# Attention, soft MoE and squared-ReLU FFN on one core: two steps written at another place in the last stage

## The chip, the core and the metric

The kernel runs on one core of a Trainium2 chip. The core has five engines that matter here: TensorE (PE in the profile; its weight loads are listed apart as PEld), VectorE (DVE), ScalarE (ACT), GpSimd (POOL) and SyncE (SP, which issues the DMAs). The metric is the device time of one execution in microseconds (us), lower is better. Before the change three runs took 477.72, 477.78 and 479.6 us; their median is 477.78.

## The reference, cut to what matters

```python
# stage 1: chunked attention, stage 2: soft MoE (slot_out is 32 rows, c is 3072 x 32)
x = c @ slot_out                       # 3072 x 512
# stage 3: squared-ReLU FFN, d_model 512, d_ff 2048
h = x @ w_in
r = np.maximum(h, 0.0)
g = s * (r * r) + b
return g @ w_out
```

The first two stages end in 32 slot rows and in the weights `c` of every token over them. So `x @ w_in` is `c @ (slot_out @ w_in)`, and the kernel never forms `x`: it forms m = slot_out @ w_in (32 x 2048, kept in `mpack`) and multiplies the transposed `c` (kept in `cpack`) by it.

## The kernel before, in words

All names below are those of the last stage, the squared-ReLU FFN. Its work is cut into 128 items. An item n is one block of 384 tokens and one block f of 128 columns of w_in. For each item:

- `emit_h(n)` (line 825) is one matmul on PE: 128 columns of `mpack` times 384 columns of `cpack`, into a PSUM tile with the tag `s`.
- `emit_relu(n)`, `emit_sq(n)`, `emit_ghi(n)` (lines 831, 835, 839) run on ACT: relu out of PSUM, the square, and a rounded copy `ghi`.
- `emit_g(n)` (line 842) runs on DVE: the rest `glo` = square minus `ghi`.
- `emit_o` and `emit_o2` (lines 877 and 889) are nine matmuls on PE, three token tiles times `ghi`·`w_hi`, `glo`·`w_hi` and `ghi`·`w_lo`. They come LA = 3 items behind the item's own `ghi`.

PSUM tiles have tags. `s` has two banks that are handed out in turn, to the h of every item and to the sums of m (below). A bank is given out again once its last reader is done, so an h waits for the reader of the tile two before it:

```python
bufs = {"s": 2, "g": 2}.get(tag, 1)
```

Beside the items the stage converts weights. w_out arrives as raw words and is split into `w_hi[f]` and `w_lo[f]`; blocks of w_in are converted in the same way. One conversion has a step on ACT (`stage_a`, line 579) and up to six on DVE (`stage_d`: lines 589, 591, 593, 600, 791, 793), and for w_out the cast to `w_hi` between them (`stage_w` on ACT, line 798; for f = 0 line 941 on DVE). DVE's first step reads what ACT's wrote.

m is formed in blocks of 512 columns. Block 0 is formed ahead of the items by `m_part` (line 688) in three column ranges: `ha` (128 columns, bank `mpa`), `hb` (128, `mpb`) and `hc` (256, `mpc`). `m_split` brings a range into `mpack`: a cast on ACT (line 817), then on DVE the rest for the lower 64 rows (line 818). Blocks 1 to 3 are formed within the items 4, 26 and 34 (`M_AT`): in item n `emit_m` runs 8 or 12 matmuls in four column groups into one `s` bank (line 806) and copies it to `mps` on ACT (line 808). In item n + 1 `emit_m2` adds the four column groups with one fp32 matmul against a stacked identity (line 812, listed as two) into another `s` bank, and splits that into `mpack` (lines 817, 818).

There is no planner: every engine takes its instructions in the order in which the code writes them, and waits where an operand or a bank is not ready. Within one item of the loop PE's order is `emit_h(n)`, the nine o matmuls of earlier items, then the matmul of `emit_m` or `emit_m2` if there is one. For the items 5 to 7 the h stands behind the o matmuls. Raw tiles of w_in and w_out come by DMA into a ring of three; the first tile of w_out is the last transfer that the head of this stage needs.

Of the kernel before, what the change touches and what calls it, by code (L numbers as in the profile page):

```python
# [35 lines left out]
def kernel(  # L36
# [30 lines left out]
    def psum(tag, shape):  # L67
        bufs = {"s": 2, "g": 2}.get(tag, 1)
        return ps.tile(shape, F32, tag=tag, name=tag, bufs=bufs)
# [48 lines left out]
    with tc.manual_schedule():  # L118
# [457 lines left out]
        def cv_act(key, i, w):  # L576
            h, lf, a = (cvs[i][:, j, :] for j in range(3))
            cv[key] = h, lf, a, w
            nc.scalar.activation(out=h, in_=w[:, :, 1].bitcast(F32), func=AF.Copy, scale=2.0 ** -112)
# [22 lines left out]
        def wi_src(fb, j):  # L602
            w = wt["wi", 2 * fb + j // 2].rearrange("p (k f t) -> p (k f) t", k=KD, t=2)
            return w[:, 512 * (j % 2):512 * (j % 2) + 512, :]
# [81 lines left out]
        def m_part(mp, kcs, cols):  # L686
            for kc in kcs:
                nc.tensor.matmul(out=mp[:, cols], lhsT=soT4[:, kc].rearrange("p r s -> p (r s)"),
                                 rhs=wis_a[kc // 2][:, kc % 2, cols], start=(kc == 0), stop=(kc == KD - 1))
# [56 lines left out]
        M_AT = (4, 26, 34)  # L746
# [26 lines left out]
        def stage_a(k):  # L773
            key = cq.get(k)
            if key:
                if key[0] == "i":
                    w = wi_src(key[1], key[2])
                else:
                    w = wt[raw_of[key]].rearrange("p (f d t) -> p f d t", f=2, t=2)[:, key[1] % 2]
                cv_act(key, k // 2 % 2, w)  # L780

        def stage_d(k, j):
            key = cq.get(k)
            if key:
                h, lf, a, w = cv[key]
                if j < 3:
                    cv_dve(key, j)
                elif j == 3:
                    cv_low(key, lf if key[0] == "o" else wi_dst([wis_l[:, 0:2], wis_l[:, 2:4]], key))
                elif key[0] == "o" and j == 4:  # L790
                    nc.vector.tensor_tensor(out=a, in0=a, in1=w_hi[key[1]].bitcast(F32), op=ALU.subtract)
                elif key[0] == "o":
                    nc.vector.tensor_tensor(out=w_lo[key[1]], in0=a, in1=lf, op=ALU.add)
# [6 lines left out]
        def emit_m(fb):  # L800
            wis = wis_b if fb % 2 else wis_a
            mp = psum("s", [128, 512])
            for lo in range(1 if fb == 1 else 2):
                for kc in range(KD):
                    lhsT, rhs = (soTb[:, kc, :], wis_l[:, kc, :]) if lo else (soT4[:, kc, 0, :], wis[kc // 2][:, kc % 2, :])
                    nc.tensor.matmul(out=mp[32 * kc:32 * kc + 32, :], lhsT=lhsT, rhs=rhs,
                                     start=(lo == 0), stop=(lo == 1 or fb == 1))
            nc.scalar.copy(out=mps, in_=mp)

        def emit_m2(fb):  # L810
            mr = psum("s", [128, 512])
            nc.tensor.matmul(out=mr, lhsT=stks_all, rhs=mps, start=True, stop=True)
            m_split(mr, 512 * fb, slice(0, 512))

        def m_split(mp, base, cols):
            m = mpack[:, base + cols.start:base + cols.stop]
            nc.scalar.copy(out=m, in_=mp[:, cols])
            nc.vector.tensor_tensor(out=m[64:128], in0=mp[64:128, cols], in1=m[64:128].bitcast(F32), op=ALU.subtract)  # L818

        def emit_h(n):  # L820
            if n >= len(items):
                return
            (b, _, _), f = items[n]
            hq = psum("s", [128, UT])
            nc.tensor.matmul(out=hq, lhsT=mpack[:, 128 * f:128 * f + 128], rhs=cpack[:, b * UT:(b + 1) * UT],  # L825
                             start=True, stop=True)
            h_t[n] = hq

        def emit_relu(n):
            if n < len(items):  # L830
                nc.scalar.activation(out=r_g[n % 2], in_=h_t.pop(n), func=AF.Relu)  # L831
# [5 lines left out]
        def emit_ghi(n):  # L837
            if n < len(items):
                nc.scalar.copy(out=ghi_g[n % (LA + 2)], in_=r2_g[n % 2])  # L839
# [28 lines left out]
        def emit_o(n, parts=(0, 1)):  # L868
            r_, f = items[n]
            ghi, glo = ghi_g[n % (LA + 2)], glo_g[n % (LA + 2)]  # L870
            if f == r_[1] and 0 in parts:
                o_t[r_] = [psum(("pt", "x", "xt", "lp", "g", "g")[3 * place[r_] + t], [128, DM]) for t in range(NTU)]
            if n == len(items) - 1:
                return
            for gt in [(ghi, glo)[x] for x in parts]:
                for t in range(NTU):
                    nc.tensor.matmul(out=o_t[r_][t], lhsT=gt[:, 128 * t:128 * t + 128], rhs=w_hi[f],  # L877
                                     start=(f == r_[1] and gt is ghi), stop=False)

        def emit_o2(n):  # L880
            r_, f = items[n]
            b, f0, f1 = r_
            ghi, glo = ghi_g[n % (LA + 2)], glo_g[n % (LA + 2)]
            for t in range(NTU):
                o = o_t[r_][t]
                if n == len(items) - 1:
                    for gt in (ghi, glo):
                        nc.tensor.matmul(out=o, lhsT=gt[:, 128 * t:128 * t + 128], rhs=w_hi[f], start=False, stop=False)
                nc.tensor.matmul(out=o, lhsT=ghi[:, 128 * t:128 * t + 128], rhs=w_lo[f], start=False, stop=(f == f1 - 1))  # L889
                if f == f1 - 1:  # L890
                    if b < 4 and f0 == 0:
                        to = part[b][t] if b < 2 else os_early(b - 2, t)
                        if t == 1:
                            nc.scalar.activation(out=to, in_=o, func=AF.Copy, scale=sbt[:, 0:1])
                        else:
                            nc.vector.tensor_scalar(out=to, in0=o, scalar1=sbt[:, 0:1], scalar2=None, op0=ALU.mult)  # L896
                    else:
                        os_ = os_g[t]
                        nc.vector.scalar_tensor_tensor(out=os_, in0=o, scalar=sbt[:, 0:1], in1=part[b][t] if f0 else bias,
                                                       op0=ALU.mult, op1=ALU.add)  # L900
                        store(b, t, os_)
# [12 lines left out]
        def stages(n, *js):  # L914
            for j in js:
                stage_d(n, j)
# [10 lines left out]
            cp[k](out=soT4[:, 2 + k, :, 16:32].rearrange("p r (e j) -> p r e j", e=4),  # L927
                  in_=sot[:, k:k + 1, :, 0:4].to_broadcast([128, 4, 4, 4]))
        m_part(mpb, (0, 1), hb)
        stage_a(0)  # L930
        m_part(mpa, (2, 3), ha)
        m_split(mpa, 0, ha)
        m_part(mpb, (2, 3), hb)
        stages(0, 0)
        m_split(mpb, 0, hb)
        emit_h(0)
        emit_h(1)
        mpc = psum("g", [128, 512])
        m_part(mpc, range(KD), hc)
        stages(0, 1)  # L940
        nc.vector.tensor_copy(out=w_hi[0], in_=cv[cq[0]][2])
        act(0)
        emit_g(0)
# [25 lines left out]
        for n in range(LA + 1, len(items) + LA + 1):  # L969
            if n > 7:  # L970
                emit_h(n)
            m = n - LA - 1
            ends = 0 <= m and items[m][1] == items[m][0][2] - 1
            late = m + 1 < len(items) and m + 1 == 2 * HF + 1
            if ends or late:
                emit_o2(m)
            if 1 < m + 1 < len(items):
                emit_o(m + 1)
            if m > 1 and not ends and not late:
                emit_o2(m)  # L980
            if LA + 1 < n <= 7:
                emit_h(n)
            if n == 6:
                nc.vector.tensor_copy(out=soTb, in_=soT4[:, :, 0, :])
            emit_relu(n)
            emit_sq(n)
            stage_a(n + 1)
            emit_ghi(n)
            if n in M_AT:
                emit_m(M_AT.index(n) + 1)  # L990
            if n - 1 in M_AT:
                emit_m2(M_AT.index(n - 1) + 1)
            if LA + 1 < n <= len(items):
                emit_g(n - 1)
            stage_d(n, 1)
            stage_w(n)
            stages(n, 2, 3)
            stages(n - 1, 4, 5)
            stage_d(n + 1, 0)
            if 48 <= n < 64:  # L1000
                for i in (2 * n - 96, 2 * n - 95):
                    wsum_add(i)
            if n == 64:
                colsum()
            if 65 <= n < 77:
                add_bias(n - 65)
            while wnext[0] < len(order) and last_use.get(order[wnext[0] - NRG], -1) <= n:
                load_w(1)
# [72 lines left out]
```

## Time and profile before

| | before |
|---|---|
| median of 3 runs | 477.78 us |
| the profiled execution's own time | 481.1 us |
| its span in the trace | 479.3 us |
| PE busy (3960 matmuls) | 455.8 us, 95% |
| PE weight loads | 342.8 us, 72% |
| DVE busy | 309.6 us, 65% |
| ACT busy | 307.6 us, 64% |
| granted TensorE clock, mean | 0.999 |

The profiled execution took 3.3 us longer than the median of the runs. The span in the trace is 1.8 us shorter than that execution. The matmuls of one item are pipelined: their listed durations overlap, and it is the distance between the starts that says how fast PE goes. The items run from 171.9 us to the end.

### The profile page before, as it was taken

To read this page: it belongs to the slowest core of one execution; us is meant where nothing else is said; L and a number is where in the kernel's file an instruction comes from. 1 tells how busy PE (TensorE), PEld (TensorE's weight loads), DVE (VectorE), ACT (ScalarE), POOL (GpSimd) and SP (SyncE) were. 2 spreads that over 40 slices of the span, in tenths; PEclk is the share of its full clock that TensorE was granted. 3 is DMA by queue.
4 is the path that set the end of the run, shared out by engine and by line. 5 is a ranking of instruction groups with operands and counts; after the bars stand their busy time and mean duration, and the time that the engine had idled before them with its cause. 6 is when DMAs were issued, how large, how long until landed. Compare 5 with 4: busy or idle time off the path is not lost.

```text
span 479.3 us, 10204 instructions
## 1 busy us (share of the span) xinstructions
PE 455.8 (95%) x3960; PEld 342.8 (72%) x3960; DVE 309.6 (65%) x685; ACT 307.6 (64%) x635; POOL 84.1 (18%) x154
## 2 busy tenths in 40 slices
PE   6889998999999878999999999999999999999996
PEld 5656666665545365886787888887888888888885
DVE  5768888886485867999485999985624224223232
ACT  4556665665134357998686888666666666666660
POOL 6665655560000000000000000006700000000000
PEclk9999999999999999999999999999999999999999
DMA  8999999999999932333332000003101001001011
GB/s 302 371 406 403 399 408 401 392 384 402 384 408 383 416 137 88 116 150 96 115 142 88 1 1 0 1 0 131 69 0 67 0 1 66 0 1 65 2 66 66
DMA packets 20576, 83.04 MB, mean 173 GB/s; under 512 B 2736, under 2 KB 2864, under 8 KB 14640
## 3 DMA queue, kind: packets, MB, share of 16 engines
q1 hardware_dynamic: 20528, 82.39, 44.5%
q8 instruction: 31, 0.51, 0.4%
q14 instruction: 17, 0.14, 0.1%
HBM read 76.09 MB, written 6.29 MB: 172 GB/s over the span
## 4 chain that ended last, share of the span: by engine, by line
PE 68%; DVE 12%; DMA 10%; ACT 4%; issue 2%; POOL 2%; SPq 1%; DVEq 0%; POOLq 0%; ACTq 0%
PE g L877 11%; PE lp L877 5%; PE pt L877 5%; PE x L877 5%; PE g L889 5%; PE xt L877 5%; PE s L825 4%; DMA keys<-in_w_out_dram 4%; DMA vals<-in_vm_dram 3%; PE s L630 3%; PE x L325 3%; PE lp L889 3%; PE pt L889 3%; PE xt L889 3%; PE x L889 3%; PE s L285 2%
## 5 line engine op out<-in xcount | busy, mean ns | idle before, releaser
L842 DVE TENSOR_TENSOR glo<-r,ghi 128x384 fp32r<-128x384 f32 x128 | 76.3, 600 | 81.4 <-ACT ghi L839 81.2
L831 ACT ACTIVATE r<-s 128x384 f32<-128x384 f32 x128 | 62.7, 490 | 52.7 <-PE s L825 52.4
L835 ACT ACTIVATE r<-r 128x384 f32<-128x384 f32 x128 | 67.2, 525 | 9.7 <-DVE glo L842 5.6
L839 ACT CAST ghi<-r 128x384 fp32r<-128x384 f32 x128 | 65.4, 511 | 3.4
L825 PE MATMUL s<-cpack,mpack 128*128 128x384 f32 x128 | 44.7, 352 | 1.9 <-DVE mpack L818 1.9
L301 ACT ACTIVATE seg<-seg 128x384 f32<-128x384 f32 x32 | 28.7, 897 | 19.2 <-DVE seg L312 15.3
L889 PE MATMUL g<-wlo,ghi 128*128 128x512 f32 x128 | 40.2, 394 | 0.0
L877 PE MATMUL g<-whi,ghi 128*128 128x512 f32 x126 | 39.7, 394 | 0.3 <-DVE mpack L818 0.3
L877 PE MATMUL g<-whi,glo 128*128 128x512 f32 x126 | 39.4, 393 | 0.0
L864 POOL TENSOR_TENSOR keys<-keys,bias 128x512 f32<-128x512 f32 x6 | 8.4, 1430 | 169.4 <-DVE bias L853 169.4
L263 POOL TENSOR_SCALAR keys<-keys 64x416 f32<-64x416 f32 x63 | 33.6, 533 | 14.2 <-DMA keys<-in_kq_dram 7.4
L285 PE MATMUL s<-keys 128*32 128x128 f32 x768 | 30.3, 291 | 5.0 <-POOL keys L267 4.2
L325 PE MATMUL x<-vals,seg 128*32 128x128 f32 x744 | 28.0, 275 | 3.6 <-DMA vals<-in_vm_dram 2.9
L825 PEld LDWEIGHTS s<-cpack,mpack 128*128 128x128 f32 x128 | 23.9, 188 | 9.5 <-DVE mpack L818 2.0
L325 PEld LDWEIGHTS x<-vals,seg 128*32 128x32 f32 x744 | 20.5, 109 | 13.3 <-DVE seg L309 4.6
L889 PEld LDWEIGHTS g<-wlo,ghi 128*128 128x128 f32 x128 | 24.0, 188 | 5.2
L877 PEld LDWEIGHTS g<-whi,glo 128*128 128x128 f32 x126 | 23.7, 188 | 5.4
L285 PEld LDWEIGHTS s<-keys 128*32 128x32 f32 x768 | 19.5, 113 | 11.0 <-POOL keys L267 6.5
L319 ACT COPY seg<-pt 128x384 f32<-128x384 f32 x32 | 15.2, 476 | 18.5 <-PE pt L317 17.6
L877 PEld LDWEIGHTS g<-whi,ghi 128*128 128x128 f32 x126 | 23.7, 188 | 4.4 <-DVE mpack L818 0.7
L877 PE MATMUL lp<-whi,ghi 128*128 128x512 f32 x63 | 25.5, 404 | 0.9 <-DVE vals L896 0.9
L877 PE MATMUL pt<-whi,glo 128*128 128x512 f32 x64 | 25.3, 395 | 0.7 <-DVE glo L842 0.7
(255 smaller groups left out, 990.6 us busy)
## 6 DMA issues: line engine op xcount, KB each, us to landing
seg<-in_w_dram SPq DMA_DIRECT2D x27, 1024.0 KB, 8.5
keys<-in_kq_dram SPq DMA_DIRECT2D x32, 396.0 KB, 7.3
vals<-in_vm_dram SPq DMA_DIRECT2D x64, 192.0 KB, 6.6
keys<-in_w_in_dram SPq DMA_DIRECT2D x5, 1024.0 KB, 5.1
keys<-in_w_out_dram SPq DMA_DIRECT2D x5, 1024.0 KB, 4.9
out_dram<-os SPq DMA_DIRECT2D x18, 256.0 KB, 2.1
vals<-in_w_in_dram SPq DMA_DIRECT2D x3, 1024.0 KB, 7.7
vals<-in_w_out_dram SPq DMA_DIRECT2D x3, 1024.0 KB, 4.8
```

The costliest lines, as they stand in the source:

```text
L263: (nc.vector if h and u == 0 else nc.gpsimd).tensor_scalar(out=stream(kz[rows, h], 0, CH), in0=k[rows, UT * h:UT * h + (NCU + 1) * CH].rea ...
L285: nc.tensor.matmul(out=o, lhsT=qt[:, 32 * c:32 * c + 32], rhs=kz[:, :, at:at + WIN], start=True, stop=not (first or last))
L301: nc.scalar.activation(out=p_r[u], in_=sm_r[u].rearrange("p t h (a r) -> p t r (h a)", a=2), func=AF.Exp, scale=scale)
L319: nc.scalar.copy(out=pts_r[u], in_=pt)
L325: nc.tensor.matmul(out=xp[32 * r:32 * r + 32, t], lhsT=pts_r[u][:, 32 * c:32 * c + 32], rhs=vbuf[u // 2 % 2][:, u % 2, :, 64 * c:64 * c + ...
L825: nc.tensor.matmul(out=hq, lhsT=mpack[:, 128 * f:128 * f + 128], rhs=cpack[:, b * UT:(b + 1) * UT], start=True, stop=True)
L831: nc.scalar.activation(out=r_g[n % 2], in_=h_t.pop(n), func=AF.Relu)
L835: nc.scalar.activation(out=r2_g[n % 2], in_=r_g[n % 2], func=AF.Square)
L839: nc.scalar.copy(out=ghi_g[n % (LA + 2)], in_=r2_g[n % 2])
L842: nc.vector.tensor_tensor(out=glo_g[n % (LA + 2)], in0=r2_g[n % 2], in1=ghi_g[n % (LA + 2)].bitcast(F32), op=ALU.subtract)
L877: nc.tensor.matmul(out=o_t[r_][t], lhsT=gt[:, 128 * t:128 * t + 128], rhs=w_hi[f], start=(f == r_[1] and gt is ghi), stop=False)
L889: nc.tensor.matmul(out=o, lhsT=ghi[:, 128 * t:128 * t + 128], rhs=w_lo[f], start=False, stop=(f == f1 - 1))
```

## The change

Two places in the code are written in another order; no instruction is added or removed, and on PE, POOL and SP the order stays as it was.

```diff
         m_part(mpb, (0, 1), hb)
-        stage_a(0)
         m_part(mpa, (2, 3), ha)
         m_split(mpa, 0, ha)
         m_part(mpb, (2, 3), hb)
-        stages(0, 0)
+        stage_a(0)
         m_split(mpb, 0, hb)
         emit_h(0)
         emit_h(1)
         mpc = psum("g", [128, 512])
         m_part(mpc, range(KD), hc)
-        stages(0, 1)
+        stages(0, 0, 1)
...
+            if n in M_AT:
+                emit_m(M_AT.index(n) + 1)
+            if n - 1 in M_AT:
+                emit_m2(M_AT.index(n - 1) + 1)
             emit_relu(n)
             emit_sq(n)
             stage_a(n + 1)
             emit_ghi(n)
-            if n in M_AT:
-                emit_m(M_AT.index(n) + 1)
-            if n - 1 in M_AT:
-                emit_m2(M_AT.index(n - 1) + 1)
```

The first piece is DVE's order at the head of the stage. `mpack<-pt` and `mpack<-lp` are the rests of the ranges `ha` and `hb`; L589, L591 and the cast to `whi` (line 941 before, 940 now) are the first conversion of w_out.

```order
 L818 TENSOR_TENSOR mpack<-pt,mpack 64x128
-L589 TENSOR_SCALAR seg_99<-seg_99 128x512
 L818 TENSOR_TENSOR mpack<-lp,mpack 64x128
-L591 SCALAR_TENSOR_TENSOR seg_99<-keys,seg_99 128x512
-L941 CAST whi_2622<-seg_99 128x512
+L589 TENSOR_SCALAR seg_99<-seg_99 128x512
+L591 SCALAR_TENSOR_TENSOR seg_99<-keys,seg_99 128x512
+L940 CAST whi_2622<-seg_99 128x512
```

Both rests now stand ahead of the conversion. On ACT the conversion's step (L579) has likewise moved by one, from ahead of the cast of `ha` to between the casts of `ha` and `hb`.

The second piece is ACT's order in items 4 and 5. The three instructions relu, square and `ghi` of item 4 (r_2658, r_2660, ghi_2666) stood just ahead of its first row before.

```order
 L808 COPY mps_2657<-s 128x512
+L831 ACTIVATE r_2658<-s 128x384
+L835 ACTIVATE r_2660<-r_2658 128x384
+L839 CAST ghi_2666<-r_2660 128x384
 L798 CAST whi_2624<-seg_99 128x512
-L831 ACTIVATE r_2659<-s 128x384
-L835 ACTIVATE r_2661<-r_2659 128x384
-L579 ACTIVATE keys<-keys 128x512
-L839 CAST ghi_2662<-r_2661 128x384
 L817 CAST mpack<-s 128x512
+L831 ACTIVATE r_2659<-s 128x384
+L835 ACTIVATE r_2661<-r_2659 128x384
```

The copy to `mps` now stands ahead of item 4's three instructions, and the cast to `mpack` ahead of item 5's four.

The third piece is ACT's order in items 26 and 27 (r_2658 to ghi_2663 belong to item 26, r_2659 to ghi_2664 to item 27).

```order
-L831 ACTIVATE r_2658<-s 128x384
-L835 ACTIVATE r_2660<-r_2658 128x384
-L839 CAST ghi_2663<-r_2660 128x384
 L808 COPY mps_2657<-s 128x512
-L831 ACTIVATE r_2659<-s 128x384
-L835 ACTIVATE r_2661<-r_2659 128x384
-L579 ACTIVATE seg_99<-keys 128x512
-L839 CAST ghi_2664<-r_2661 128x384
+L831 ACTIVATE r_2658<-s 128x384
+L835 ACTIVATE r_2660<-r_2658 128x384
+L839 CAST ghi_2663<-r_2660 128x384
 L817 CAST mpack<-s 128x512
```

Copy and cast have moved ahead of the relu of the same item here too; items 34 and 35 show the same.

## Rows read from the trace of the kernel before

**Rows 1.** The page's chain that ended last: share of the span by engine.
```profile
PE 68%; DVE 12%; DMA 10%; ACT 4%; issue 2%; POOL 2%; SPq 1%; DVEq 0%; POOLq 0%; ACTq 0%
```

**Rows 2.** Stretches: length, then busy us (instructions) by engine, clock, DMA.
```profile
171.00:190.00 19.00, 15.99 (x67) 10.99 (x68) 15.21 (x29) 14.98 (x32) 0.00 (x0) 1.00 0.19 71
190.00:215.00 25.00, 25.00 (x112) 20.57 (x111) 24.41 (x48) 21.70 (x45) 0.00 (x0) 1.00 0.36 127
...
222.00:300.00 78.00, 78.00 (x355) 61.90 (x354) 63.54 (x118) 62.06 (x126) 0.00 (x0) 1.00 0.17 61
```

**Rows 3.** Timeline, ACT, head: start, length, instruction, [idle before <- what ended it].
```profile
170.74 0.66 ACT L579 ACTIVATE seg<-keys 128x512 f32<-128x512 f32 x1 [2.38 <-DMA keys<-in_w_out_dram]
171.31 0.25 ACT L817 CAST mpack<-pt 128x128 fp32r<-128x128 f32 x1
```

**Rows 4.** Timeline, DVE, head of the stage.
```profile
171.59 0.29 DVE L818 TENSOR_TENSOR mpack<-pt,mpack 64x128 fp32r<-64x128 f32 x1 [2.58 <-ACT mpack L817]
...
172.37 0.29 DVE L818 TENSOR_TENSOR mpack<-lp,mpack 64x128 fp32r<-64x128 f32 x1
172.70 0.69 DVE L591 SCALAR_TENSOR_TENSOR seg<-keys,seg 128x512 int32<-128x512 int32 x1
...
174.04 0.56 DVE L842 TENSOR_TENSOR glo<-r,ghi 128x384 fp32r<-128x384 f32 x1 [0.19 <-ACT ghi L839]
```

**Rows 5.** Timeline, ACT, items 3 to 5.
```profile
179.54 0.48 ACT L831 ACTIVATE r<-s 128x384 f32<-128x384 f32 x1
...
181.60 0.47 ACT L831 ACTIVATE r<-s 128x384 f32<-128x384 f32 x1
...
183.09 0.58 ACT L808 COPY mps<-s 128x512 f32<-128x512 f32 x1
184.14 0.62 ACT L798 CAST whi<-seg 128x512 fp32r<-128x512 f32 x1 [0.47 <-DVE seg L591]
...
186.57 0.58 ACT L817 CAST mpack<-s 128x512 fp32r<-128x512 f32 x1
```

**Rows 6.** Timeline, PE and PEld, 180 to 189 us.
```profile
180.07 0.16 PEld L806 LDWEIGHTS s<-vals,keys 128*32 128x32 f32 x8 [0.40 <-ACT r L831]
...
183.72 1.13 PE L812 MATMUL s<-mps,stk 128*128 128x512 f32 x2 [0.82 <-ACT mps L808]
...
188.50 0.50 PE L877 MATMUL pt<-whi,glo 128*128 128x512 f32 x1 [0.70 <-DVE glo L842]
```

**Rows 7.** Timeline, DVE, item 5.
```profile
184.60 0.69 DVE L600 SCALAR_TENSOR_TENSOR seg<-keys,seg 128x512 f32<-128x512 uint32 x1
187.18 0.69 DVE L818 TENSOR_TENSOR mpack<-s,mpack 64x512 fp32r<-64x512 f32 x1 [1.89 <-ACT mpack L817]
```

**Rows 8.** Timeline, PE and ACT, items 26 to 28.
```profile
235.87 0.40 PE L806 MATMUL s<-seg 128*32 128x512 bf16 x4
236.19 0.44 PE L825 MATMUL s<-cpack,mpack 128*128 128x384 f32 x1
236.31 0.59 ACT L808 COPY mps<-s 128x512 f32<-128x512 f32 x1 [1.70 <-PE s L806]
...
236.47 0.40 PE L877 MATMUL pt<-whi,ghi 128*128 128x512 f32 x1
...
236.79 0.50 ACT L831 ACTIVATE r<-s 128x384 f32<-128x384 f32 x1
...
238.53 1.02 PE L812 MATMUL s<-mps,stk 128*128 128x512 f32 x2
...
239.57 0.39 PE L877 MATMUL lp<-whi,ghi 128*128 128x512 f32 x1
239.59 0.59 ACT L817 CAST mpack<-s 128x512 fp32r<-128x512 f32 x1 [0.79 <-PE s L812]
```

**Rows 9.** Instructions of line 825: ns min/median/max, first and last start.
```profile
L825 PEld LDWEIGHTS s<-cpack,mpack x128: 186/188/190, 171.9 to 465.9; 128*128 128x128 f32 x128
```

**Rows 10.** Timeline, PE, the end of the first run of items.
```profile
219.68 0.50 PE L877 MATMUL lp<-whi,ghi 128*128 128x512 f32 x1 [0.86 <-DVE vals L896]
```

## The prediction

> **What bounds the kernel now.** I read the chain of waits first, because it says which engine's time sets the end: 68% of it is PE, 12% DVE, 10% DMA [rows 1]. An average over a whole span hides stages, so I then cut the last stage into stretches [rows 2]. From 171 to 190 us no engine is full: PE is busy for 15.99 of 19 us, DVE for 15.21. From 190 to 215 us PE is full (25.00 of 25) and DVE nearly (24.41). From 222 to 300 us PE is full again (78.00 of 78), and it stays so. The timelines say what ends each idle piece. At the head ACT waits until 170.74 for the first tile of w_out [rows 3]. In items 4 and 5 PE and DVE wait for ACT's copy and cast of m: PE 0.82 and, by way of `glo`, 0.70 us [rows 6], DVE 1.89 us [rows 7]. At 219.68 PE waits for DVE once more [rows 10]. After that an instruction moved on ACT can only matter if PE comes to wait for it.
>
> The granted clock is 1.00 in all these stretches [rows 2], the ones with PE's waits included, so I give the clock no term.
>
> **The head.** Before, ACT began the first conversion step at 170.74 and the cast of `ha` at 171.31, 0.57 later [rows 3]. DVE took the rest of `ha` at 171.59, 0.28 after the cast, and the rest of `hb` at 172.37, between two conversion steps; the next step began at 172.70, and `glo` at 174.04 after 0.19 of idle [rows 4]. Now the cast of `ha` is done while ACT waits for the DMA, and the cast of `hb` takes its place at 171.31. DVE takes the rest of `hb` at about 171.59, where that of `ha` stood. The second rest thus leaves the series: 172.70 − 172.37 = 0.33 us. The 0.19 of idle goes too, because h and relu of item 0 no longer wait for a cast behind the DMA. Together 0.5 us. The DMA itself is not sooner, so there is no more to gain: ACT's step still starts at 170.74. What follows on DVE up to item 4 is nearly a closed series, so the 0.5 us is carried on. Bounds: 0 (if item 0's `ghi` is late again) to 0.7; I take 0.5.
>
> **Items 4 and 5.** All times are before's; the 0.5 is counted above. ACT's relu of item 4 began at 181.60 [rows 5]. The matmuls of `emit_m` had run from 180.07 with nothing behind them on that bank [rows 6], so the copy to `mps` can take this place: 181.60 to 182.19 instead of 183.09. Then relu, square and `ghi` of item 4 end about 0.58 later than they did, still ahead of the cast of `whi` at 184.14, which waits for DVE [rows 5]: nothing late there. PE's sum (L812) no longer waits for `mps`: its 0.82 goes, less some 0.1 because h of item 5 now needs the later relu. The cast to `mpack` follows `whi` directly. That one ends at 184.14 + 0.62 = 184.76, so the cast begins at about 184.7 in place of 186.57 and ends at about 185.3. DVE's rest can start when L600 ends, 184.60 + 0.69 = 185.29, in place of 187.18: 1.89 us less [rows 7]. The `glo` behind it, for which PE waited 0.70 at 188.50 [rows 6], moves by the same. relu, square, conversion step and `ghi` of item 5 come 0.58 later; DVE's conversion series is far enough behind (its next first step needs the rest, a `glo` and two w_out steps first) that nobody waits for them.
>
> Is the 1.89 worth its size at the end? Over 190 to 215 us PE runs without a gap, so it gains only if it enters that run sooner. It does: its idle pieces before 190 are the 0.82, the 0.70 and the restart behind them, and the 0.5 of the head. At 219.68 DVE sets PE's start [rows 10], and DVE is sooner by 0.5 + 1.89. Gain at the two early places: 2.4 us. Bounds: 0.5 (only the head) to 3.3 (if the 0.86 at 219.68 goes as well).
>
> **Items 26 and 34.** Here PE is full, and ACT waits for PE, not PE for ACT [rows 2, 8]. PE's order is h(26), nine o, the matmuls of `emit_m`, h(27), nine o, L812, h(28). The `s` banks go in turn: h(26) one, `emit_m` the other, h(27) the first again, L812 the other, h(28) the first. So h(27) waits for relu(26), and h(28) for relu(27). Before, both were long done. Now relu(26) stands behind the copy, and the copy behind the last matmul of `emit_m`.
>
> First wait. The copy starts at 236.31 as before. The next relu starts 0.48 later (236.79) [rows 8]. A bank is free 0.53 after its relu's start: relu at 179.54 [rows 5], the weight load that waited for it at 180.07 [rows 6]. So h(27) starts at 236.31 + 0.48 + 0.53 = 237.32 instead of 236.19: 1.13 us. Queued behind it are the nine o matmuls, and nothing else can go ahead.
>
> Second wait. L812 to the cast is 239.59 − 238.53 = 1.06, cast to relu 0.48, relu to bank 0.53, h to the next o 236.47 − 236.19 = 0.28: together 2.35 us from L812 to the next o. Before it was 239.57 − 238.53 = 1.04 [rows 8], since h(28) was pipelined into the sum. So 1.31 us.
>
> That is 2.44 us per place. Items 34 and 35 have the same pattern (the copy's idle of 1.70 stands there again), so 4.9 us. The copy's and cast's own gain here is worth nothing: PE's order puts their next use nine matmuls or more later. DVE's rest of m comes 1.1 later together with all PE work, and DVE has idle time there (63.54 of 78 us busy [rows 2]). Bounds: 0, if the relus were never needed in time, to 6, if a start after each wait costs another 0.25 us.
>
> In the row at 180.07 the weight load itself was held until relu was done [rows 6]. The Trainium skill, TensorE: Matmul & The Clock Gate, section Step-by-step: what each phase is for, says that the queue can pull a weight load ahead of running matmuls. By that rule the load of h (0.188 us [rows 9]) would lie inside each of the four waits, at most 0.75 us less, and the sum would be +1.8 instead of +2.5. I go by the row.
>
> **The sum.** −0.5 − 1.9 + 4 waits (2 × 1.13 + 2 × 1.31 = 4.9) = +2.5 us. Against the profiled execution: 481.1 + 2.5 = 483.6. The median of the runs lies 3.3 below that execution; I put the same difference on it: 477.78 + 2.5 = 480.3 us.
>
> **Rivals.**
> - The early gain is lost in the full stretch. PE has no gap from 190 to 215 [rows 2]; if its restart there is set by something that did not move, only the head's 0.5 counts: 477.78 + 4.9 − 0.5 = 482.2. Against it: every idle piece of PE that the rows name before 190 ends with something that moves. 0.14.
> - Only one wait per late place. If h(28) finds its bank free (say, relu(27) gets done before L812 has drained), 2 × 1.31 falls away: 477.7. Against it: ACT's order puts the cast, which needs L812's result, ahead of that relu. 0.14.
> - Faster: the late places cost nothing. The mechanism would be that PE has slack there, the stretch being paced by DVE's conversions (63.54 of 78 us busy, in bursts). Then only the 2.4 shows: 475.4; it decides itself at h(27), 1.13 us or none. Against it: PE busy for 78.00 of 78. 0.06.
> - The change does less at the head than it says, since the first tile's DMA rules: 0.5 less, 480.8. It lies within the forecast's own range.
>
> **How the numbers follow.** Forecast 0.60 (own range 479.2 to 481.4), the three rivals 0.14, 0.14, 0.06, and 0.06 for a mixture. About 0.5% (2.4 us) is what a measurement of this kernel can tell from no change, so the borders are 475.4 and 480.2; the forecast sits on the upper one, and I split its 0.60 into 0.30 slower and 0.30 within. Slower: 0.30 + 0.14 + some 0.05 of the mixture = 0.49. Faster: 0.04, since that rival lies on the lower border. Within: 0.47. Range 477.6 to 482.4: it takes in both middle rivals and leaves out the faster one.
>
> **What would show it.** In the trace after: the rest of `hb` at about 171.6 and `glo` 0.5 sooner; no idle of DVE ahead of its next L818, and PE's L812 in item 5 without a wait for `mps`; PE's run without gaps beginning some 2.4 us sooner than 190; then at the two late places h waiting for ACT's relu, twice each, with 1.1 and 1.3 us. Wrong would be: a PE without these four waits, or an early part that arrives at 222 us with less than 2 us in hand.

## The result and the profile after

The changed kernel takes 480.65 us (median of 21 runs), the kernel before 478.0 us (21 runs). The ratio is 1.0052, with a 95% interval from 1.0035 to 1.0068: 2.5 us slower, between 1.7 and 3.3. The prediction was 480.3 us, 2.5 us more than the 477.78 it started from.

The profiled execution after is one of the shorter ones: 479.52 us, span 477.7, which is less than the 479.3 of before. The spans of two single executions can't be set against each other here, because the weight transfers end at different times: PE was done with the range `ha` of m at 169.64 us in the trace of before and at 167.19 in that of after. So I compare intervals within each trace.

**The early items.** ACT and DVE in items 4 and 5 of the changed kernel (start, length, engine, line, instruction, idle time before it):

```profile
177.66 0.57 ACT L808 COPY mps<-s 128x512 f32<-128x512 f32 x1
178.12 0.49 ACT L831 ACTIVATE r<-s 128x384 f32<-128x384 f32 x1
...
180.20 0.62 ACT L798 CAST whi<-seg 128x512 fp32r<-128x512 f32 x1 [0.48 <-DVE seg L591]
180.72 0.58 ACT L817 CAST mpack<-s 128x512 fp32r<-128x512 f32 x1
```

```profile
180.66 0.69 DVE L600 SCALAR_TENSOR_TENSOR seg<-keys,seg 128x512 f32<-128x512 uint32 x1
181.36 0.69 DVE L818 TENSOR_TENSOR mpack<-s,mpack 64x512 fp32r<-64x512 f32 x1
```

The rest of m follows the conversion step without a gap; its 1.89 us of idle in [rows 7] is gone. PE's sum no longer waits either; the row that had 0.82 in [rows 6] now reads:

```profile
178.80 1.02 PE L812 MATMUL s<-mps,stk 128*128 128x512 f32 x2
```

From the first `w_lo` on DVE to h(8) on PE it takes 11.53 us, and 13.43 in the trace of before: 1.90 us less.

**The late items.** ACT in items 26 and 27, then PE, in the changed kernel; they answer to [rows 8]:

```profile
230.52 0.59 ACT L808 COPY mps<-s 128x512 f32<-128x512 f32 x1 [3.54 <-PE s L806]
231.00 0.50 ACT L831 ACTIVATE r<-s 128x384 f32<-128x384 f32 x1
...
234.56 0.59 ACT L817 CAST mpack<-s 128x512 fp32r<-128x512 f32 x1 [1.96 <-PE s L812]
235.04 0.50 ACT L831 ACTIVATE r<-s 128x384 f32<-128x384 f32 x1
```

```profile
230.08 0.40 PE L806 MATMUL s<-seg 128*32 128x512 bf16 x4
231.16 0.45 PE L825 MATMUL s<-cpack,mpack 128*128 128x384 f32 x1 [0.68 <-ACT mps L808]
...
233.50 1.02 PE L812 MATMUL s<-mps,stk 128*128 128x512 f32 x2
235.59 0.44 PE L825 MATMUL s<-cpack,mpack 128*128 128x384 f32 x1 [1.07 <-ACT r L831]
235.88 0.39 PE L877 MATMUL lp<-whi,ghi 128*128 128x512 f32 x1
```

Both waits of h are there. The second is as forecast: from L812 to the next o 235.88 − 233.50 = 2.38 us (forecast 2.35, before 1.04). The first is not: h(27) starts at 231.16, while relu(26), which began at 231.00, still runs. What it waited for is the copy, which ends at 230.52 + 0.59 = 231.11.

**The full stretches.** PE is busy for every microsecond from 184.2 to 209, as it was from 190 to 215 in [rows 2], and the clock is still 1.00 (columns: stretch, length, then busy time and instructions of PE, PEld, DVE, ACT, POOL, clock, DMA):

```profile
184.20:209.00 24.80, 24.80 (x111) 20.41 (x110) 24.21 (x47) 22.08 (x46) 0.00 (x0) 1.00 0.37 129
216.00:294.00 78.00, 74.50 (x336) 58.27 (x335) 60.17 (x111) 58.89 (x120) 0.00 (x0) 1.00 0.18 62
```

The later stretch lost 78.00 − 74.50 = 3.5 us of PE that was full before: the four waits (2 × 0.68 + 2 × 1.07). The idle time is counted from the listed ends of pipelined matmuls; by the starts of the h the waits cost more, 4.2 us (the late items alone, below). The wait at the end of the first run [rows 10] stands as it was:

```profile
213.87 0.50 PE L877 MATMUL lp<-whi,ghi 128*128 128x512 f32 x1 [0.85 <-DVE vals L896]
```

### The profile page after: what moved, and what is told of

It is laid out like the page before. It is cut to its first block, busy times and chain, and to the rows that moved or that the text cites. A ratio compares the mean times of both kernels' runs of the same rounds, so it can differ in the third digit from the quotient of the medians.

```text
span 477.7 us, 10206 instructions
## 1 busy us (share of the span) xinstructions
PE 456.7 (96%) x3960; PEld 342.3 (72%) x3960; DVE 310.1 (65%) x685; ACT 308.7 (65%) x635; POOL 84.4 (18%) x154
## 4 chain that ended last, share of the span: by engine, by line
PE 69%; DVE 13%; DMA 8%; ACT 4%; issue 3%; SPq 2%; POOL 1%; DVEq 0%; POOLq 0%; ACTq 0%
PE g L877 11%; PE lp L877 5%; PE pt L877 5%; PE x L877 5%; PE g L889 5%; PE xt L877 5%; PE s L825 4%; DMA seg<-in_w_dram 4%; PE s L630 3%; PE x L325 3%; DMA vals<-in_vm_dram 3%; PE lp L889 3%; PE pt L889 3%; PE xt L889 3%; PE x L889 3%
## 5 line engine op out<-in xcount | busy, mean ns | idle before, releaser
L877 PE MATMUL pt<-whi,ghi 128*128 128x512 f32 x64 | 25.6, 400 | 0.0
```

## The experiments

Ratios are to the kernel before on the same chip, with 95% intervals; 0.001 is 0.48 us. All leave the computation whole.

**The early items alone**

```diff
+            def sum_m(copy, cast):
+                if copy and n in M_AT:
+                    emit_m(M_AT.index(n) + 1)
+                if cast and n - 1 in M_AT:
+                    emit_m2(M_AT.index(n - 1) + 1)
+
+            sum_m(n < 8, n < 8)
             emit_relu(n)
...
             emit_ghi(n)
...
+            sum_m(not (n < 8), not (n < 8))
```

> Only items 4 and 5 have the sum over m's column groups ahead of relu and square; items 26, 27, 34, 35 and the head as before. Theory A: DVE's idle of 1.89 us ahead of its rest of m goes and is kept to the end: 1.9 us less. Rival (PE is full from 190 to 215 us and takes the gain back): within 0.3 us of before.

Measured: 476.25 us, ratio 0.9959 (0.9944 to 0.9973), so 2.0 us less (1.3 to 2.7). The first `w_lo` on DVE and the row of h(7) and h(8) on PE (h(8) starts 0.18 behind h(7)), first in the trace of before, then in this one:

```profile
176.75 0.69 DVE L793 TENSOR_TENSOR wlo<-seg 128x512 fp32r<-128x512 f32 x1
...
190.01 0.51 PE L825 MATMUL s<-cpack,mpack 128*128 128x384 f32 x2
```

```profile
174.08 0.69 DVE L793 TENSOR_TENSOR wlo<-seg 128x512 fp32r<-128x512 f32 x1
...
185.44 0.51 PE L825 MATMUL s<-cpack,mpack 128*128 128x384 f32 x2
```

From the first `w_lo` to h(8), 13.43 us in the trace of before, it takes 11.54: 1.89 us, the very idle time of the row in [rows 7]. From there on every interval between the h of two items is that of before, within 0.05 us. The rival is refuted: PE enters its full run sooner and keeps it.

**The late items alone**

```diff
+            sum_m(n > 8, n > 8)
             emit_relu(n)
...
+            sum_m(not (n > 8), not (n > 8))
```

> Only items 26, 27, 34 and 35 have the sum ahead of relu and square; items 4 and 5 and the head as before. Theory A: at each of the two places h(n+1) waits for the copy to mps (0.75 us more than before, as in the profile of the changed kernel) and h(n+2) for a relu behind the cast (1.3 us): 4.2 us more. Theory B (the prediction as written: both wait for a relu): 4.9 us more. Rival (PE has slack there): no difference.

Measured: 482.7 us, ratio 1.0095 (1.0070 to 1.0120), 4.5 us more (3.3 to 5.7). In its trace h(26) to h(29) takes 11.11 us instead of 9.02, and h(34) to h(37) too: 2 × 2.09 = 4.2. Here are h(26) and h(29), in the trace of before and in this one:

```profile
232.64 0.34 PE L825 MATMUL s<-cpack,mpack 128*128 128x384 f32 x1
...
241.66 0.33 PE L825 MATMUL s<-cpack,mpack 128*128 128x384 f32 x1
```

```profile
230.83 0.34 PE L825 MATMUL s<-cpack,mpack 128*128 128x384 f32 x1
...
241.94 0.34 PE L825 MATMUL s<-cpack,mpack 128*128 128x384 f32 x1
```

PE's waits from 225 to 270 us there (engine, line <- releaser: us in total, times, longest):

```profile
PE s L825 <- ACT r L831: 2.1, 2, 1.1
PE s L825 <- ACT mps L808: 1.4, 2, 0.7
```

Two waits per place, one ended by the copy. The interval holds the forecast's 4.9 as well; it is the trace that decides for 4.2.

**Copy alone, cast alone, at the late items**

```diff
+            sum_m(n > 8, False)
             emit_relu(n)
...
+            sum_m(not (n > 8), not (False))
```

> Only the copy to mps of items 26 and 34 stands ahead of relu; the cast to mpack of items 27 and 35, the early items and the head as before. Theory A (two separate waits per place, the first ended by the copy): h of items 27 and 35 starts 0.75 us later, h of items 28 and 36 follows the sum at once: 1.5 us more than before. Rival (the first wait is only the first half of one delay and the second comes with it): about 4 us more.

and, in another kernel:

```diff
+            sum_m(False, n > 8)
             emit_relu(n)
...
+            sum_m(not (False), not (n > 8))
```

> Only the cast to mpack of items 27 and 35 stands ahead of relu; the copy of items 26 and 34, the early items and the head as before. Theory A: h of items 27 and 35 as before; 2.35 us instead of 1.04 from the sum to the next o: 2.6 us more than before. Rival: about 4 us more, or none because the copy's earlier place had caused the wait.

Measured: copy alone 479.27 us, ratio 1.0029 (1.0012 to 1.0046), 1.4 us more; cast alone 480.14 us, 1.0047 (1.0032 to 1.0062), 2.2 us more. PE's waits, first with the copy alone, then with the cast alone, from 215 to 270 us:

```profile
PE s L825 <- ACT mps L808: 1.4, 2, 0.7
PE lp L877 <- DVE vals L896: 0.8, 1, 0.8
```

```profile
PE s L825 <- ACT r L831: 2.1, 2, 1.1
PE lp L877 <- DVE vals L896: 0.9, 1, 0.9
```

h(26) to h(29) takes 9.78 and 10.32 us, 0.76 and 1.30 more than 9.02. Their sum, 2.06, is what both together cost (2.09). So the two waits are independent, and each belongs to the instruction that was put ahead of relu.

**Behind relu, but ahead of the square**

```diff
             emit_relu(n)
+            if n in M_AT:
+                emit_m(M_AT.index(n) + 1)
+            if n - 1 in M_AT:
+                emit_m2(M_AT.index(n - 1) + 1)
             emit_sq(n)
             stage_a(n + 1)
             emit_ghi(n)
```

> In every item of the loop the sum over m's column groups stands behind relu but ahead of the square, the conversion step and ghi; the head as before. Theory A (only relu's place behind copy and cast costs, because it frees the bank): no wait of h at items 27, 28, 35, 36; in item 5 DVE's rest of m starts 1.4 us sooner than before instead of 1.9: 1.4 us less than before. Rival (what costs is ACT as a whole, square and ghi coming late): about as slow as the changed kernel, 2 to 4 us more than before less the early gain.

Measured: 476.79 us, ratio 0.9976 (0.9953 to 0.9998), 1.2 us less. h(26) to h(29) takes 9.02 us as before: no wait at the late items, although square and `ghi` still stand behind copy and cast. So only relu's place costs there. The early items keep 1.5 of their 1.9 us (13.43 to 11.90 from `w_lo` to h(8)); DVE waits a little:

```profile
183.33 0.69 DVE L818 TENSOR_TENSOR mpack<-s,mpack 64x512 fp32r<-64x512 f32 x1 [0.36 <-ACT mpack L817]
```

**The early cast alone**

```diff
+            sum_m(False, n < 8)
             emit_relu(n)
...
+            sum_m(not (False), not (n < 8))
```

> Only the cast to mpack of item 5 stands ahead of relu; the copy of item 4 and all else as before. Theory A (DVE's idle is set by the cast's place on ACT, not by PE's wait for the copy): PE still waits 0.8 us for mps, the sum ends at 184.8 on before's clock, the cast follows, DVE's rest starts at about 185.4 instead of 187.18: 1.8 us less than before. Rival (PE's wait of 0.82 for the copy is what counts): about 0.2 us less or none, and the copy's place would bring the rest.

Measured: 476.42 us, ratio 0.9969 (0.9952 to 0.9985), 1.5 us less. DVE's idle shrinks to 0.21 us, while PE still waits 0.8 us for the copy:

```profile
181.31 0.69 DVE L818 TENSOR_TENSOR mpack<-s,mpack 64x512 fp32r<-64x512 f32 x1 [0.21 <-ACT mpack L817]
```

```profile
PE s L812 <- ACT mps L808: 0.8, 1, 0.8
PE lp L877 <- DVE vals L896: 0.7, 1, 0.7
```

It shows how a DVE gain reaches the end where PE was not sooner by as much: h(8) comes 1.0 us sooner after `w_lo`, and h(8) to h(21), the stretch with PE's wait for L896, takes 30.52 us, and 31.17 in the trace of before. Together 1.7. DVE sets that point, as [rows 10] said.

**The head alone**

```diff
-        stage_a(0)
         m_part(mpa, (2, 3), ha)
         m_split(mpa, 0, ha)
         m_part(mpb, (2, 3), hb)
-        stages(0, 0)
+        stage_a(0)
         m_split(mpb, 0, hb)
...
-        stages(0, 1)
+        stages(0, 0, 1)
```

> Only the head's edit: the first conversion step of w_out behind the splits of ha and hb; the loop as before. Theory A (the gain depends on when the first tile of w_out lands): where the tile lands behind PE's matmuls of ha, 0.5 us less; where it lands before them, as in the profile of the changed kernel (landed 166.70, PE done 167.2), ACT's step now waits for the cast of ha and two rests stand ahead of the conversion on DVE, 0.3 us more. Over the runs -0.5 to +0.4. Theory B (the prediction): always 0.5 us less, 477.5 where before is 478.0.

Measured: 477.68 us, ratio 0.9993 (0.9977 to 1.0008): no difference that can be told, and an interval that rules out neither theory. The traces are sharper. Here are ACT's rows at the head, first of this kernel, then of the kernel with the early items alone, whose head is that of before:

```profile
167.17 0.27 ACT L817 CAST mpack<-pt 128x128 fp32r<-128x128 f32 x1 [1.31 <-PE pt L688]
167.34 0.67 ACT L579 ACTIVATE seg<-keys 128x512 f32<-128x512 f32 x1
```

```profile
168.06 0.67 ACT L579 ACTIVATE seg<-keys 128x512 f32<-128x512 f32 x1 [0.86 <-DMA keys<-in_w_out_dram]
168.63 0.25 ACT L817 CAST mpack<-pt 128x128 fp32r<-128x128 f32 x1
...
169.74 0.49 ACT L831 ACTIVATE r<-s 128x384 f32<-128x384 f32 x1 [0.52 <-PE s L825]
```

In the second, the tile had landed and ACT's step had begun 0.42 us before PE was done with `ha` (168.48). ACT's conversion step then fits into ACT's wait for PE. With the edit it stands behind that wait: what DVE saves is given back by ACT. From the end of `ha` on PE to the first `w_lo` on DVE it takes 5.62 us with the edit (this kernel, the changed one and the last of this section) and 5.60 to 5.63 without it, in six profiles of kernels with the old head and the old loads. So neither the 0.5 us less of Theory B nor the 0.3 us more of Theory A is there where the tile lands early. Among the profiles with the old head and the old loads only that of before has 7.12, because there the tile landed late: ACT waited until 170.74 [rows 3], 1.10 us after `ha` was done.

**The tile made to land late**

```diff
+        order[npre], order[npre + 1] = order[npre + 1], order[npre]
```

> The first two tiles of w_out are loaded in exchanged order, so that the tile of the first conversion lands some 2.5 us later, clearly behind PE's matmuls of ha; all else as before. Both theories: from the start of ACT's first conversion step to the start of the first w_lo on DVE 6.0 us, as in the profile of before (170.74 to 176.75). It is the base for the next run.

> The same exchanged loads, with the head's edit. Theory A (the head's edit gains only where the tile lands late): 5.5 us from ACT's first conversion step to the first w_lo, 0.5 less than with the old order. Rival (the edit gains nothing in any case): 6.0 us again.

There is one execution of each, so it is the traces that count. ACT at the head, old order, then the edited one (all lines are one higher in these kernels):

```profile
171.08 0.66 ACT L580 ACTIVATE seg<-keys 128x512 f32<-128x512 f32 x1 [3.37 <-DMA keys<-in_w_out_dram]
171.64 0.26 ACT L818 CAST mpack<-pt 128x128 fp32r<-128x128 f32 x1
...
172.82 0.49 ACT L832 ACTIVATE r<-s 128x384 f32<-128x384 f32 x1 [0.76 <-PE s L826]
```

```profile
167.90 0.27 ACT L818 CAST mpack<-pt 128x128 fp32r<-128x128 f32 x1 [1.31 <-PE pt L689]
170.49 0.66 ACT L580 ACTIVATE seg<-keys 128x512 f32<-128x512 f32 x1 [2.32 <-DMA keys<-in_w_out_dram]
171.06 0.25 ACT L818 CAST mpack<-lp 128x128 fp32r<-128x128 f32 x1
171.21 0.50 ACT L832 ACTIVATE r<-s 128x384 f32<-128x384 f32 x1
```

From ACT's conversion step to the first `w_lo` it takes 6.11 us with the old order and 5.42 with the edit: 0.7 us less (0.5 expected). In both, ACT's step waits for the tile, so both times count from its landing, and from h(8) on the intervals between the h are the same: the 0.7 is kept. The edit does what the prediction worked out, where the tile lands late. The two single times, 481.58 and 480.27 us, can't show 0.7 us by themselves.

**The head and the early items, without the late ones**

```diff
-        stage_a(0)
         m_part(mpa, (2, 3), ha)
...
-        stages(0, 0)
+        stage_a(0)
         m_split(mpb, 0, hb)
...
-        stages(0, 1)
+        stages(0, 0, 1)
...
+            sum_m(n < 8, n < 8)
             emit_relu(n)
...
+            sum_m(not (n < 8), not (n < 8))
```

> The head's edit as in the change, and the sum ahead of relu in items 4 and 5 alone; items 26, 27, 34, 35 as before. Theory A (2.0 us from the early items, 0 from the head where the first tile of w_out lands 2.5 us behind the last tile ahead of it, 0.5 where it lands 4 us behind): 2.0 to 2.4 us less than before. Rival (head and early items share one gain): less than either alone promises, 1.5 us or so less.

Measured: 476.32 us, ratio 0.9963 (0.9947 to 0.9979), 1.8 us less (1.0 to 2.5). It is not told apart from the early items alone (0.9959). Both are faster than the kernel before and than the changed one; the simpler edit, the early items alone, is the version to keep.

## Why the prediction was right, point by point

- **The total** was right in sign, size and way: 480.3 forecast, 480.65 measured, the difference to before 2.5 both times. But two of its terms were off and nearly cancel. By the intervals of the traces the sum is 0 (head) − 1.9 (early) + 4.2 (late) = +2.3; the forecast had −0.5 − 1.9 + 4.9 = +2.5. That the total fits so closely is in part luck. The two profiles agree with the sum: from the end of `ha` on PE to the end of the span it takes 309.7 us before and 310.6 after, and 1.5 us of the former are the late tile (7.12 against 5.62, the head alone).
- **The early items** are right as worked out. DVE's idle of 1.89 us [rows 7] went, nothing else became late, PE's full run began sooner, and the gain was there at the end. The first rival (gain lost in the full stretch) is refuted by the early items alone.
- **The head**, 0.5 us, is the step that was mis-sized. It took the profile of before for the usual execution, although that execution was 3.3 us longer than the median. There ACT waited for the DMA until 1.10 us after PE was done with `ha` [rows 3]. In the six other profiles with the old head and the old loads the tile lands before that, and the edit is worth nothing (5.62 against 5.60 to 5.63 us from `ha` to `w_lo`). The bound of 0 was given, but for another reason. The rival with 0.5 us less at the head (480.8) thus came true in size, but not because the tile's transfer sets the pace there: it is PE's end of `ha` that ACT then waits for. By the prediction's own sign of being wrong (less than 2 us in hand from the early part) the early part fell just short, 1.9 us, for want of the head's 0.5.
- **The late items** cost 2.09 us per place instead of 2.44. The second wait was right (1.30 against 1.31), and so were its parts: 1.06 us from sum to cast, 0.48 to relu, 0.55 to the bank. The first was mis-sized (0.76 against 1.13), since its step "the `s` banks go in turn" failed: h(27) got the bank that the copy to `mps` frees, and not that of relu(26). It starts at 231.16, just behind the end of the copy (231.11), while relu(26) runs until 231.50. So the two banks are not always handed out in turn, as the prediction and the description of the kernel have it, and an h does not always wait for the reader of the tile two before it. How the bank is chosen is not shown. The written order of the readers does not explain it by itself. At the second wait the rest of m (L818), the last reader of the sum's bank, is written ahead of relu(27), and yet h(28) starts at 235.59, when relu(27) is done (235.54) and that rest still runs (until 235.87):

```profile
235.18 0.69 DVE L818 TENSOR_TENSOR mpack<-s,mpack 64x512 fp32r<-64x512 f32 x1 [3.97 <-ACT mpack L817]
```

In each of these waits, in the changed kernel and in those with the copy, the cast or both moved at the late items, the h got the bank whose last reader was done first.

- **The weight load.** In the trace after, the weight load of the waiting h is held with it:

```profile
231.16 0.19 PEld L825 LDWEIGHTS s<-cpack,mpack 128*128 128x128 f32 x1 [1.39 <-ACT mps L808]
235.59 0.19 PEld L825 LDWEIGHTS s<-cpack,mpack 128*128 128x128 f32 x1 [1.90 <-ACT r L831]
```

It starts with its matmul, at 231.16 and at 235.59, in both waits. So the load was not taken ahead in the waits, as in the row of before [rows 6]. The Trainium skill, TensorE: Matmul & The Clock Gate, section Step-by-step: what each phase is for, says that a load can be pulled ahead of running matmuls. Where no bank is waited for the trace agrees (the load of h(29) at 237.71, its matmul at 237.94); where the load's own instruction waits for the bank, no run shows it. That the forecast less the four loads (4.9 − 0.75) lies near the measured 4.2 us is chance: the difference comes from the bank of the first wait.

- **The other rivals.** "Only one wait per place" and "the late places cost nothing" are refuted by the copy alone and the cast alone: 0.76 and 1.30 us, each there by itself, and additive. The sign "h waiting for ACT's relu, twice each" held for the second wait only; the first ends with the copy.

## What to carry to other kernels

Before an instruction is moved ahead on an engine, ask what the instruction that it passes gives free: here a relu that was early on ACT returned the PSUM bank of the next item, and half a microsecond of work put ahead of it cost PE 0.8 to 1.3 us each time. The same edit gained 1.9 us where DVE was the late engine and lost 2.1 us per place where PE was, so an edit in a loop is priced for each item on which it acts, and can be applied to those alone. A wait for a transfer that one profile shows is checked in a second profile before a gain is built on it.

## What the runs showed of the hardware that was not expected

The landing of the weight transfers moves by microseconds between executions. PE was done with `ha` between 166.87 and 169.64 us in the profiles of kernels that don't differ in PE's work up to that point, a spread of 2.8 us, which is as large as the effect of the whole change. In the profile of before the tile of w_out landed 4.0 us behind the tile ahead of it, in the nine others with the same loads 2.5 us. Other traces have such a late transfer at another place: in that of after it is the next tile of w_out (169.66 − 166.70 = 2.96 us), in that with the copy alone at the late items a tile of an earlier weight (158.30 − 154.71 = 3.59 us). So which transfer is late differs from one execution to the next; why it is late stays open. PE's own intervals are steady beside that: from h(37) to the last h it took 204.21 to 204.23 us in every profile.
